# Other ranks for the planner over opening and first sweep, a shorter cost for four turns of tokens, and the second quarter of the tokens loaded second

## The chip, the cores and the metric

The kernel runs on one core of one Trainium2 chip. The metric is the device time of one execution in microseconds (us), as the median of several runs; the profile is of one execution more. The engines are TensorE (PE: matmuls and transposes), VectorE (DVE), ScalarE (ACT), GpSimd (POOL) and SyncE (SP), which here issues DMAs.

## What is computed

A two-way attention between tokens and states, and a feed-forward network over what both read:

```python
# x: 8 x 8 x 512 x 64 (batch, heads, tokens, D), state: 8 x 8 x 32 x 64, scale = 1/8
a  = softmax(scale * x @ state.T);  xread = a @ state      # tokens read states
a2 = softmax(scale * state @ x.T);  sread = a2 @ x         # states read tokens
rows = concatenate([xread, sread])                         # 8 * (512 + 32) = 4352 rows of 512
h = rows @ w_in                                            # 512 -> 2048
g = h * clip(h + 3, 0, 6) / 6
out = g @ w_out                                            # 2048 -> 512
```

Everything comes and goes as 32-bit floats; the inner products are split into parts of which three matmuls each are summed.

## The kernel before

The work is cut into units: a sweep over the eight batches b0 to b7 with the first half of the network's width, two units for all states' rows, and a second sweep over the batches with the other half. Each unit has eight steps. A step is a `first` (L1245: the matmuls L1053, for the opening's steps L1274, into a bank `ps_h`), an ACT step (`relu`, L1295), a DVE step (the product, L1298, which reads `ps_h` and so sets when that bank is free), the split of the result into a high and a low part (`g_hi` on ACT, L402, `g_lo` on DVE, L403), and later its `second` (L1343: L1053 or, unsplit, L1355), which adds into four banks `acc`.

The weights of the network arrive in two-byte pieces that are put together: a DMA at L479, a cast on ACT into `tops` (L492) and a join on DVE (L497); `w_out` is then split (L524 on ACT, L526 on DVE).

The opening does the attention of b0, since nothing can run before it. The tokens of b0 come as four quarters of two heads each, q0 to q3, on SP (`load_x`, L601), are copied into `xb` (DVE, L603), turned on TensorE (L732), copied back by ACT (L737) and multiplied with the turned states (L796): q0 and q1 into one bank of scores, q2 and q3 into another. Each bank gets a softmax on DVE and ACT: maximum L811, subtraction L813, exponential L815, sum L816, two small steps L818 and L819, scaling L820. Only when both are through does TensorE turn the result (L828), ACT copy it (L835) and the first main matmul (L1274) run. Beside it runs the states' side: `wprime` (L630, the states times `w_in`, copied by ACT at L681) and the states' own softmax (maximum L904 and L906 on DVE, exponential L908 on ACT, L911 and L913 on DVE). The tokens of the next batch come later as sixteen turned loads (`load_turned`, L617) and are transposed on DVE (L722).

What sets the order of all this is `Plan`: each operation is added with its engine, a cost, what it reads and writes and its slots. `Plan.order` (L166) then goes through time with one clock per engine, and among the operations that could start within 0.3 of the soonest it takes the one of the lowest rank. The ranks are the table `RANKS` (L25 to L132), 2592 numbers, one for each operation. `Plan.issue` (L263) emits the operations in that order, and each engine runs its own in that order on the chip. Ahead of the first main matmul it also puts idle transposes (L1660) into the gaps that TensorE has by the planned clock, one for each 0.13 of a gap. So a changed cost changes the clock, the order and the count of idle transposes.

Of the kernel before, what the change touches and what calls it, by code (L numbers as in the profile page):

```python
# [279 lines left out]
def tile_state_attention_then_hardswish_ffn(  # L280
# [72 lines left out]
    def T(cost, rank, do, reads=(), writes=(), after=()):  # L353
        return plan.add("T", cost, rank, do, reads, writes, after)
# [1336 lines left out]
```

## Time and profile before

| what | us |
|---|---|
| median of 3 runs (637.45 to 638.91) | 637.8 |
| the profiled execution | 637.48 |
| its span | 635.7 |
| TensorE busy in the span | 627.8 |
| DVE busy | 520.5 |
| ACT busy | 344.3 |

The span is the time from the first to the last instruction that the profile shows; the granted clock of TensorE is 1.00 all along. A busy TensorE has its idle transposes counted in. Waits are read from the time that an engine sat idle ahead of an instruction, with the engine and line that ended it. In timelines, matmuls of one row overlap a little, so that two starts give a better pitch than a duration does.

### The profile page before, as it was taken

The page shows a single profiled execution, that of the slowest core. Times are in us where ns is not written, and L with a number is a line of the kernel's source. Part 1 is how long each engine was busy: PE and PEld are TensorE (multiplying, and loading weights), DVE is VectorE, ACT ScalarE, POOL GpSimd, SP SyncE. Part 2 cuts the span into 40 slices and gives each one's busy share as a digit, 9 for nine tenths or more (in the row PEclk, how much of TensorE's full clock was granted, in tenths as well). Part 3 has the DMA queues.
Part 4 walks back from the last instruction along what each step waited for, and adds up shares of the span by engine and source line. Part 5 has one row for each costly group of instructions (what it writes and reads, how often), then busy time and mean ns, then how long its engine had stood idle before and what let it go on. Part 6 is the DMA issues. An engine that isn't in the chain of part 4 may idle for free.

```text
span 635.7 us, 11438 instructions
## 1 busy us (share of the span) xinstructions
PE 627.8 (99%) x4381; PEld 525.7 (83%) x4381; DVE 520.5 (82%) x947; ACT 344.3 (54%) x611; POOL 18.1 (3%) x21
## 2 busy tenths in 40 slices
PE   8999999999999999999999999999999999999997
PEld 6466777777777778778888888899999999999996
DVE  5999997978988798885568738999979899988773
ACT  5875565546545554444456657665446455554431
POOL 0000000000000000000000000000000000001010
PEclk9999999999999999999999999999999999999999
DMA  8998895966687694540313868323526225522244
GB/s 293 283 219 141 247 176 158 203 169 184 129 198 167 168 211 107 134 101 31 70 67 106 286 207 231 99 48 87 133 36 164 35 35 129 104 35 34 34 67 99
DMA packets 168261, 86.18 MB, mean 136 GB/s; under 512 B 128528, under 2 KB 152976, under 8 KB 168080
## 3 DMA queue, kind: packets, MB, share of 16 engines
q1 hardware_dynamic: 164240, 77.47, 47.3%
q0 software_dynamic: 3824, 7.87, 8.5%
q8 instruction: 34, 0.56, 0.4%
q14 instruction: 19, 0.16, 0.1%
q10 hardware_dynamic: 144, 0.13, 0.1%
HBM read 50.84 MB, written 34.60 MB: 134 GB/s over the span
## 4 chain that ended last, share of the span: by engine, by line
PE 93%; DMA 2%; DVE 2%; SPq 1%; ACT 1%; issue 0%; ACTq 0%
PE acc L1053 31%; PE acc L1165 24%; PE ps_h L1053 23%; PE ps_s L1053 7%; PE ps_s L630 2%; PE acc L1355 1%; PE ps_s L1491 1%; DMA raw<-in_moe_w_out_dram 1%; PE ps_h L1010 1%; DMA raw<-in_moe_w_in_dram 1%; SPq L617 1%; PE acc L1491 1%; PE ps_h L630 1%; DMA raw<-in_x_dram 0%; SPq L601 0%
## 5 line engine op out<-in xcount | busy, mean ns | idle before, releaser
L1053 PE MATMUL acc<-w_out_hi,g_hi 128*128 128x512 f32 x296 | 118.2, 399 | 0.5 <-ACT g_hi L402 0.5
L1053 PE MATMUL acc<-w_out_lo,g_hi 128*128 128x512 f32 x296 | 115.5, 390 | 0.0
L1053 PE MATMUL acc<-w_out_hi,g_lo 128*128 128x512 f32 x296 | 115.3, 390 | 0.0
L1165 PE MATMUL acc<-w_out_hi,tmp 128*128 128x256 f32 x360 | 87.9, 283 | 0.0
L1295 ACT ACTIVATE g<-ps_h,three 128x512 f32<-128x512 f32 (+1 forms) x80 | 51.3, 647 | 57.8 <-PE ps_h L1053 51.4
L1298 DVE SCALAR_TENSOR_TENSOR g<-g,ps_h 128x512 f32<-128x512 f32 (+1 forms) x80 | 50.1, 629 | 27.9 <-ACT g L1295 27.2
L1053 PEld LDWEIGHTS acc<-w_out_hi,g_hi 128*128 128x128 f32 x296 | 55.6, 188 | 19.6 <-issue 7.0
L1165 PE MATMUL acc<-w_out_hi,g_lo 128*128 128x256 f32 x240 | 68.0, 283 | 0.0
L1165 PE MATMUL acc<-w_out_lo,g_hi 128*128 128x256 f32 x240 | 67.9, 283 | 0.0
L1165 PE MATMUL acc<-w_out_hi,g_hi 128*128 128x256 f32 x240 | 67.9, 283 | 0.0
L1053 PE MATMUL ps_h<-aT_hi,wp_hi 128*128 128x512 f32 (+1 forms) x188 | 67.6, 360 | 0.0
L1165 PEld LDWEIGHTS acc<-w_out_hi,tmp 128*128 128x128 f32 x360 | 66.3, 192 | 0.3
L1053 PE MATMUL ps_h<-aT_lo,wp_hi 128*128 128x512 f32 (+1 forms) x188 | 66.5, 354 | 0.0
L1053 PE MATMUL ps_h<-aT_hi,wp_lo 128*128 128x512 f32 (+1 forms) x188 | 66.4, 353 | 0.0
L1053 PEld LDWEIGHTS acc<-w_out_hi,g_lo 128*128 128x128 f32 x296 | 55.6, 188 | 12.2 <-DVE g_lo L403 0.4
L1053 PEld LDWEIGHTS acc<-w_out_lo,g_hi 128*128 128x128 f32 x296 | 55.6, 188 | 10.7 <-issue 0.3
L402 ACT CAST g_hi<-G 128x512 fp32r<-128x512 f32 (+1 forms) x64 | 38.2, 605 | 46.8 <-PE acc L1165 38.7
L402 ACT CAST g_hi<-g 128x512 fp32r<-128x512 f32 (+1 forms) x74 | 42.7, 585 | 26.3 <-DVE g L1298 15.5
L403 DVE TENSOR_TENSOR g_lo<-g,g_hi 128x512 fp32r<-128x512 f32 (+1 forms) x74 | 46.8, 643 | 8.7 <-ACT g_hi L402 6.7
L1165 PE MATMUL acc<-w_out_lo,tmp 128*128 128x256 f32 x180 | 50.9, 283 | 0.0
L403 DVE TENSOR_TENSOR g_lo<-G,g_hi 128x512 fp32r<-128x512 f32 (+1 forms) x64 | 42.2, 669 | 6.1 <-ACT g_hi L402 5.5
L1165 PEld LDWEIGHTS acc<-w_out_hi,g_hi 128*128 128x128 f32 x240 | 46.0, 192 | 0.7
(179 smaller groups left out, 1272.8 us busy)
## 6 DMA issues: line engine op xcount, KB each, us to landing
out_dram<-ot SPq DMA_DIRECT2D x8, 1024.0 KB, 4.9
W<-G SPq DMA_DIRECT2D x16, 512.0 KB, 4.1
out_dram<-ot POOLq DMA_DIRECT2D x15, 512.0 KB, 5.9
raw<-in_x_dram SPq DMA_DIRECT2D x112, 64.0 KB, 2.8
xb<-in_x_dram SPq DMA_DIRECT2D x28, 256.0 KB, 4.8
raw<-in_moe_w_out_dram SPq DMA_DIRECT2D x11, 511.8 KB, 5.4
wp_lo<-W SPq DMA_DIRECT2D x40, 128.0 KB, 2.8
raw<-in_moe_w_in_dram SPq DMA_DIRECT2D x8, 511.0 KB, 5.6
```

What stands on the lines that cost most here:

```text
L402: first = S_(cost, rank, lambda: nc.scalar.copy(hi(), src()), reads, [writes[0]], after)
L403: V(cost, rank, lambda: nc.vector.tensor_tensor(lo(), src(), hi().bitcast(F32), op=ALU.subtract), [*reads, writes[0]], [writes[1]])
L617: nc.sync.dma_start(t[rows, i].rearrange("t (a c) -> t a c", c=NS), x[b, 4 * g + 2 * i + u, :, k * NS : (k + 1) * NS].rearrange("(a t) c - ...
L630: nc.tensor.matmul(out[u][cols, :], made["stT", b][rows, cols], moving(q)[rows], start=True, stop=True,)
L1010: nc.tensor.matmul(bank(pr)[cols, u * D : (u + 1) * D], e2T(b, u)[:, j * P + q * NS : j * P + (q + 1) * NS], x_tile(b, True)[:, NG * q + u ...
L1053: nc.tensor.matmul(ps, l, r, start=start and k == 0, stop=stop and k == n - 1)
L1165: nc.tensor.matmul(out, left(a, l), right(b, r), start=p == 0 and z == 0 and y == 0, stop=p == FPS // 2 - 1 and y == 2, skip_group_check=True)
L1295: in_turn["g", n] = S_(cost + 0.05, rank, lambda: nc.scalar.activation(g(), bank(ps)[:, :width], AF.Relu, bias=three, scale=-1.0 if turned ...
L1298: V(cost, rank, lambda: nc.vector.scalar_tensor_tensor(g(), g(), 6.0, bank(ps)[:, :width], op0=ALU.min, op1=ALU.mult), [ps], [g_key])
L1355: nc.tensor.matmul(bank(acc), made["g_hi", n][:, js], plain_out[f][1](), start=opens, stop=closes)
L1491: nc.tensor.matmul(bank(banks[q // 2][u])[:, q % 2 * W : (q % 2 + 1) * W], st[l]()[rows, q], wp(r)[rows, q], start=y == 0, stop=y == 2, sk ...
```

## The change

The planner's cost for the turn of a quarter of the tokens (L732) becomes 0.47 instead of 0.7, and the 2592 ranks are other ones:

```diff
 RANKS = [int(k) for k in """
-2 0 8 3 33 1 18 4 38 20 28 11 21 37 40 25 31 53 58 29 36 39 43 57
...
+10 8 82 9 97 12 100 13 94 60 98 5 160 47 170 2 169 3 181 113 107 59 4 64
...
 """.split()]
...
             x_parts = [(*x_key(b), "q", q)] if b == 0 else [(*x_key(b), j) for j in range(J)]
-            T(0.7, rank, turn, x_parts, [ps], after)
+            T(0.47, rank, turn, x_parts, [ps], after)
             S_(0.6, rank, lambda q=q, ps=ps: nc.scalar.copy(xT(b, q), bank(ps)), [ps], [xT_key(b, q)])
```

The operations are the same ones, 2592 of them, with the same instructions on DVE, ACT, SP and POOL. TensorE has eight idle transposes more, 50 instead of 42: 12, 3, 1, 7, 11, 9 and 7 in the gaps of the opening, where it had 12, 4, 1, 8, 6, 3 and 8. In the second half of the order TensorE's row is the same as before.

On SP the first quarters and the weights of the opening stand in another order. The names: `ot` is the raw tile of b0's tokens, a row of two being two quarters; `early` and `raw` are pieces of the weights. Before:

```order
L601 DMA ot<-in_x_dram 128x2x256 x2
L546 DMA st_raw<-in_state_dram 128x128
L601 DMA ot<-in_x_dram 128x2x256 x2
L479 DMA raw<-in_moe_w_out_dram 128x2047
L479 DMA early_108<-in_moe_w_in_dram 128x4x511 x2
L479 DMA early_113<-in_moe_w_in_dram 128x4x1023
L479 DMA raw<-in_moe_w_out_dram 128x2047 x2
```

After:

```order
L601 DMA ot<-in_x_dram 128x2x256 x2
L546 DMA st_raw<-in_state_dram 128x128
L479 DMA early_104<-in_moe_w_in_dram 128x4x511
L601 DMA ot<-in_x_dram 128x2x256 x2
L479 DMA raw<-in_moe_w_out_dram 128x2047 x2
L479 DMA early_104<-in_moe_w_in_dram 128x4x511
L479 DMA early_133<-in_moe_w_in_dram 128x4x1023
L479 DMA early_150<-in_moe_w_out_dram 128x2047
```

What moved: q1 now goes ahead of q2, half a piece of `w_in` goes ahead of q2 and q3, and the second piece of `w_out` comes ahead of the other pieces of `w_in`. The sixteen turned loads of the next tokens (L617), of which six went ahead of a late piece of weights, all stand behind it.

On DVE this is the opening, from the last copies L603 to the first scaling L820. `early` and `raw` at L497 are the joins of `w_in` and `w_out`, L811 to L820 the two softmaxes. Before:

```order
L603 COPY xb<-ot 128x2x4x64
L497 SCALAR_TENSOR_TENSOR raw<-raw,tops 128x512
L811 TENSOR_REDUCE m_196<-ps_s 128x16
L813 TENSOR_TENSOR w_in_204<-ps_s,m_196 128x8x64
L497 SCALAR_TENSOR_TENSOR w_in_212<-early_108,tops 128x4x128
L811 TENSOR_REDUCE m_215<-ps_s 128x16
L816 TENSOR_REDUCE s_230<-w_in_204 128x16
L813 TENSOR_TENSOR w_in_204<-ps_s,m_215 128x8x64
L818 TENSOR_SCALAR s_230<-s_230 128x16
L819 RECIPROCAL s_230<-s_230 128x16
L820 TENSOR_TENSOR w_in_204<-w_in_204,s_230 128x8x64
L816 TENSOR_REDUCE s_230<-w_in_204 128x16
```

After:

```order
L811 TENSOR_REDUCE m_180<-ps_s 128x16
L813 TENSOR_TENSOR w_in_190<-ps_s,m_180 128x8x64
L603 COPY xb<-ot 128x2x4x64
L497 SCALAR_TENSOR_TENSOR w_in_207<-early_104,tops 128x4x128
L816 TENSOR_REDUCE s_215<-w_in_190 128x16
L497 SCALAR_TENSOR_TENSOR raw<-raw,tops 128x512
L818 TENSOR_SCALAR s_215<-s_215 128x16
L819 RECIPROCAL s_215<-s_215 128x16
L497 SCALAR_TENSOR_TENSOR raw<-raw,tops 128x512
L811 TENSOR_REDUCE m_239<-ps_s 128x16
L813 TENSOR_TENSOR w_in_190<-ps_s,m_239 128x8x64
L820 TENSOR_TENSOR w_in_190<-w_in_190,s_215 128x8x64
```

What moved: the first bank's maximum and subtraction come ahead of the last copy L603, and two joins of `w_out` stand between the first bank's sum and the second bank's maximum, where before one stood ahead of everything and the other, below these rows, behind both softmaxes.

On ACT this is the end of the opening, from the copies of the turned softmax (L835) to the first two `relu` (L1295). `aT_hi` is the split of these copies, `tmp` the states' exponential. Before, with numbers:

```order
L835 COPY w_in2_204<-acc1_289 128x256
L835 COPY w_in2_204<-acc0_294 128x256
L835 COPY w_in2_204<-acc1_289 128x256
L835 COPY w_in2_204<-acc0_294 128x256
L492 CAST tops_91<-early1_113 128x512
L524 CAST w_out_hi0_228<-raw_133 128x512
L402 CAST aT_hi_327<-w_in2_204 128x512 x2
L908 ACTIVATE tmp_341,r2_342<-ps_s_248,nm2_303 128x512
L1295 ACTIVATE g_349<-ps_h_318,three_89 128x512
L908 ACTIVATE tmp_351,r2_342<-ps_s_247,nm2_299 128x512
L1295 ACTIVATE g_354<-ps_h_336,three_89 128x512
```

After:

```order
L835 COPY w_in2_190<-acc1_301 128x256 x2
L835 COPY w_in2_190<-acc0_306 128x256 x2
L402 CAST aT_hi_320<-w_in2_190 128x512
L492 CAST tops_91<-raw_167 128x512
L908 ACTIVATE tmp_341,r2_342<-ps_s_259,nm2_311 128x512
L1295 ACTIVATE g_348<-ps_h_329,three_89 128x512
L908 ACTIVATE tmp_355,r2_342<-ps_s_258,nm2_332 128x512
L492 CAST tops_91<-early3_150 128x512
L1295 ACTIVATE g_371<-ps_h_345,three_89 128x512
```

What moved: one `aT` split and the split of `w_out` no longer stand ahead of the first exponential of the states L908.

On TensorE this is the place in the first sweep where the tokens of the next batch are read (L1010): a `first` (into `ps_h`), seconds (into `acc`), the read, and then the `second` of that `first`. Before, with numbers:

```order
L1053 MATMUL ps_h_693<-aT_hi_327,wp_hi_433 128x512
L1053 MATMUL ps_h_693<-aT_lo_334,wp_hi_433 128x512
L1053 MATMUL ps_h_693<-aT_hi_327,wp_lo_446 128x512
L1053 MATMUL acc0_376<-w_out_hi1_461,g_hi_609 128x512
L1053 MATMUL acc0_376<-w_out_lo1_472,g_hi_609 128x512
L1053 MATMUL acc0_376<-w_out_hi1_461,g_lo_651 128x512
L1010 MATMUL ps_s_717<-xb_110,tmp_700 32x64 x16
L1010 MATMUL ps_s_717<-xb_110,tmp_704 32x64 x16
L1053 MATMUL acc2_370<-w_out_hi1_461,g_hi_755 128x512
L1053 MATMUL acc2_370<-w_out_lo1_472,g_hi_755 128x512
L1053 MATMUL acc2_370<-w_out_hi1_461,g_lo_759 128x512
L1053 MATMUL acc3_395<-w_out_hi1_461,g_hi_755 128x512
```

After:

```order
L1053 MATMUL ps_h_658<-aT_hi_320,wp_lo_431 128x512
L1053 MATMUL acc1_374<-w_out_hi1_513,g_hi_578 128x512
L1053 MATMUL acc1_374<-w_out_lo1_532,g_hi_578 128x512
L1053 MATMUL acc1_374<-w_out_hi1_513,g_lo_618 128x512
L1053 MATMUL acc2_386<-w_out_hi1_513,g_hi_592 128x512
L1053 MATMUL acc2_386<-w_out_lo1_532,g_hi_592 128x512
L1053 MATMUL acc2_386<-w_out_hi1_513,g_lo_602 128x512
L1053 MATMUL acc1_374<-w_out_hi1_513,g_hi_592 128x512
L1053 MATMUL acc1_374<-w_out_lo1_532,g_hi_592 128x512
L1053 MATMUL acc1_374<-w_out_hi1_513,g_lo_602 128x512
L942 MATMUL ps_s_695<-ident_84,tmp_355 128x128 x4
L942 MATMUL ps_s_700<-ident_84,tmp_341 128x128 x4
```

What moved: behind the `first` stand three seconds ahead of the turn L942 (and two more behind it, ahead of the read L1010), where before one stood between the `first` and the read; the turn was ahead of the `first`.

## Rows read from the trace of the kernel before

**Rows 1.** The page: engines (busy us, share of the span, instructions), two groups (busy, mean ns).
```profile
PE 627.8 (99%) x4381; PEld 525.7 (83%) x4381; DVE 520.5 (82%) x947; ACT 344.3 (54%) x611; POOL 18.1 (3%) x21
...
L1295 ACT ACTIVATE g<-ps_h,three 128x512 f32<-128x512 f32 (+1 forms) x80 | 51.3, 647 | 57.8 <-PE ps_h L1053 51.4
L1298 DVE SCALAR_TENSOR_TENSOR g<-g,ps_h 128x512 f32<-128x512 f32 (+1 forms) x80 | 50.1, 629 | 27.9 <-ACT g L1295 27.2
```

**Rows 2.** Busy time of each engine by stretch, granted clock, DMA share, GB/s.
```profile
10.00:20.00 10.00, 8.20 (x96) 5.84 (x95) 9.37 (x18) 7.18 (x17) 0.00 (x0) 1.00 1.02 353
...
40.00:60.00 20.00, 19.47 (x182) 13.39 (x181) 18.88 (x35) 11.99 (x21) 0.00 (x0) 1.00 0.83 168
```

**Rows 3.** TensorE's waits: us in total, times, longest us.
```profile
PE acc L630 <- DVE w_in L497: 1.1, 1, 1.1
PE acc L1053 <- ACT g_hi L402: 0.5, 1, 0.5
...
PE ps_s L630 <- ACT tmp L908: 0.2, 1, 0.2
```

**Rows 4.** The chain that ended last, to 70 us: start us, us, what.
```profile
3.23 6.34 DMA raw<-in_moe_w_out_dram
...
10.46 0.69 DVE raw L497
...
17.56 0.70 DVE w_in L820
18.31 1.11 PE acc L828 x8
```

**Rows 5.** Loads L601, half w_in, w_out1: durations ns, first and last start us; landing.
```profile
L601 SPq DMA_DIRECT2D ot<-in_x_dram x4: 431/446/469, 0.7 to 2.7; - x4
...
DMA to landing us min/median/max: 2.7/3.5/4.9
...
L479 SPq DMA_DIRECT2D early<-in_moe_w_in_dram x1: 434/434/434, 3.7 to 3.7; - x1
...
DMA to landing us min/median/max: 7.2/7.2/7.2
...
L479 SPq DMA_DIRECT2D raw<-in_moe_w_out_dram x1: 1369/1369/1369, 5.9 to 5.9; - x1
...
DMA to landing us min/median/max: 10.5/10.5/10.5
```

**Rows 6.** DVE's timeline: start us, us, line and operation, idle before.
```profile
11.78 0.69 DVE L813 TENSOR_TENSOR w_in<-ps_s,m 128x512 f32<-128x512 f32 x1
12.39 0.68 DVE L497 SCALAR_TENSOR_TENSOR w_in<-early,tops 128x512 uint32<-128x512 uint32 x1
...
14.78 0.17 DVE L818 TENSOR_SCALAR s<-s 128x16 f32<-128x16 f32 x1
...
15.27 0.69 DVE L820 TENSOR_TENSOR w_in<-w_in,s 128x512 f32<-128x512 f32 x1
```

**Rows 7.** TensorE's timeline, 16 to 32 us, same columns.
```profile
16.03 0.87 PE L1660 MATMUL ps_h<-ident 128*128 128x128 f32 x6
...
20.14 3.70 PE L1274 MATMUL ps_h<-w_in,tmp 128*128 128x512 f32 x8
23.77 0.62 PE L630 MATMUL ps_s<-w_in,stT 64*32 64x256 f32 x2
...
25.17 4.77 PE L1355 MATMUL acc<-raw,g 128*128 128x512 f32 x10
...
31.25 0.66 PE L630 MATMUL ps_s<-w_in,stT 64*32 64x256 f32 x16
```

**Rows 8.** TensorE's timeline at 59 us.
```profile
59.17 0.50 PE L1053 MATMUL acc<-w_out_hi,g_hi 128*128 128x512 f32 x1 [0.52 <-ACT g_hi L402]
...
60.25 0.40 PE L1053 MATMUL acc<-w_out_hi,g_hi 128*128 128x512 f32 x1
60.48 0.40 PE L1053 MATMUL acc<-w_out_lo,g_hi 128*128 128x512 f32 x1
```

214 rows, old and new, of the table RANKS are left out of this document.

## The prediction
> **What bounds the kernel now.** I read the page first: TensorE is busy 627.8 us of a span of 635.7 [rows 1]. So only two things can move the time by much: TensorE's own work, or the few moments in which it does no useful work. The change adds no matmul of the product and takes none away, so I looked for the moments. The busy times by stretch show the first: from 10 to 20 us TensorE is busy 8.20, and part of that is idle transposes, while DVE is busy 9.37 [rows 2]. The table of TensorE's waits then shows how little is left: 1.1 us on DVE's join of `w_in`, 0.5 on an ACT split, 0.2 on an exponential of the states [rows 3]. All three places are in the part of the order that the change rewrites, the opening and the first sweep. What is not in that table is the time that TensorE spends on idle transposes, and the time that a matmul takes longer than its neighbours while it waits in the pipeline; the timeline has to give these.
>
> The chain that ended last says what the opening hangs on: the first `w_out` load (3.23 + 6.34 = 9.57 us), DVE's join at 10.46, then DVE without a gap to the scaling of the second half's softmax at 17.56, the turn back on TensorE at 18.31 [rows 4], the first of the main matmuls at 20.14 [rows 7]. The opening is thus DVE bound from the first arriving weights on, and each 0.1 us taken out of DVE's row before 17.56 would bring TensorE's 20.14 forward by as much.
>
> **Arrivals.** Loads land in the order of issue, as their summed bytes come. With 256 KB for a quarter of the tokens, 64 for the state and 512 for a `w_out` or half `w_in` load, before gives: four quarters and the state (1,088 KB) at 2.7 + 4.9 = 7.6; + w_out0 (1,600) at 9.57; + half w_in (2,112) at 3.7 + 7.2 = 10.9; after two more `w_in` loads (512 and 1,024 KB), w_out1 (4,160) at 5.9 + 10.5 = 16.4 [rows 4, 5]. That is 2,560 KB in 6.83 us, 375 KB a us. After's order is q0, q1, state, half w_in, q2, q3, w_out0, w_out1, the other half, w_in of the next. An estimate by the same bytes: half w_in at 7.6 (1,088), q2 at 8.6 (1,344), q3 at 9.6 (1,600), w_out0 at 10.9 (2,112), w_out1 at 12.3 (2,624), the other half of w_in at 13.7 (3,136). The tokens' second half (q2, q3) comes 2 to 3 us later than before, w_out1 four earlier, and w_in's first half 3.3 earlier.
>
> This rests on order of issue deciding the landing. The Trainium skill, page "DMA: Bandwidth & Descriptors", section "Queues, rings and completion order", says that descriptors are consumed in ring order but that a later transfer may complete before an earlier one. Of the loads summed here the rows show none that did; by that rule q2 and q3 could slip towards the weights behind them, and the price would be that of rival C.
>
> **The opening on DVE.** An operation on 128x512 takes a place of 0.61 us (11.78 to 12.39), the two small ones before a scaling 0.49 together (14.78 to 15.27) [rows 6], and from a landing through ACT's cast to the join it is 0.9 (9.57 to 10.46) [rows 4]. By after's order: the first half's scores are there at about 8.7, since q0 and q1 land first, so maximum and subtraction run from 8.9 on; the copy of q3 at about 10.2; join of half w_in 10.66; sum 11.26; join of w_out0 11.87; small ones; join of w_out1 at 13.2, for which DVE waits (landing at 12.3, and 0.9); the second half's maximum 13.8, subtraction 14.4; scaling of the first 15.0; join 15.6; sum 16.2; small ones; scaling of the second 17.35 to 18.05. Before had it at 17.56 + 0.70 = 18.26 [rows 4]. So early tokens buy only 0.2 us: the row is the same work, and one more join (w_out1's) stands ahead of the end. Bounds: it could be 0.6 earlier if DVE doesn't wait for w_out1 (one place of 0.61), and later by whatever w_out1's landing is late. I take **-0.2**.
>
> The eight added idle transposes cost six for 0.87 us [rows 7], 0.14 each, 1.1 in all, if nothing covers them. What covers them is the wait for DVE: by the sum above, TensorE's row (scores of the second half, half w_in product, 11 idle, the 512-wide product, half w_in product, 9 idle) ends at about 17.9, just ahead of 18.05. I cost them at nothing, with 0.2 of cover left and 1.1 at the other end.
>
> **From 20 to 30 us.** The states' product (L630) takes 23.77 to 25.17 = 1.40 us where the same sixteen matmuls later run in 0.66 [rows 7]: 0.75 lost, of which the table names 0.2 for the exponential L908 [rows 3]. ACT comes late to that: behind the copies of the opening's end it has a cast, a split of `w_out` and both splits of `aT` ahead of L908. In after the split of `w_out` and one split of `aT` stand elsewhere. The lost 0.75 should go, so that L1355 starts 0.2 + 0.75 = **0.95 earlier**. What is late next: `aT`'s other split and the join for L630 at about 28.3; by the places of 0.6 on DVE and ACT these are done 0.1 to 0.8 ahead of use, so little cover is left. Then after has three `first` with one L1355 between the second and third, and the third needs the bank of the first, which an ACT step of 647 ns and a DVE step of 629 free [rows 1]; one queued step ahead of each makes 0.3 to 0.5 us of wait. I give back **0.3**. The sixteen turned loads of the next tokens now all stand behind a weight's buffer on SP, where six went ahead of it; their readers on DVE come about when the last of them lands, so I cost that at nothing, with 0.5, the longest stall past the opening [rows 3], at the other end.
>
> **At 59 us.** TensorE waits 0.52 for ACT's split, and the step's first three matmuls take 59.17 to 60.25 = 1.08 where one step is 0.23 (60.25 to 60.48), 0.69 for three: 0.39 more, **0.9 in all** [rows 8]. Between that `first` and its own `second` before has one other second of three matmuls and the tokens' read; after has four seconds more and the turn L942, of which the 12 matmuls alone are 12 x 0.23 = 2.8 us of cover. So this goes. But DVE, which is busy 18.88 of the 20 us up to there [rows 2], is only a little ahead of TensorE, and after puts three `first` in a row right behind. The third waits for the first one's 0.65 + 0.63, which two L1053 groups of 1.38 would hide, but DVE's backlog does not. I give back **0.5** (0.1 to 0.9).
>
> **Sum.** -0.2 - 0.75 + 0.3 - 0.9 + 0.5 = -1.05. Beyond the first sweep the order is the same: nothing. The profiled execution took 637.48, 0.3 below the median 637.8 of the three runs, of which 1.8 lie around the span; 637.48 - 1.05 = 636.4. Set against the median it would be 636.75; I put it at **636.5**. What a measurement can tell from no change is 0.2%, 1.3 us: 636.5 stands on that edge, so that "faster" and "same" share the forecast.
>
> **Rivals.**
> A. The forecast, 635.8 to 637.1: 0.50.
> B. Nothing is freed: what TensorE gains at 25 us it waits for again at 28 to 33 and at 60, since DVE is nearly as full as TensorE. For: 9.37 of 10 us, and 18.88 of 20 [rows 2], and the DVE chain in [rows 4]. Against: behind the opening TensorE's waits are waits for ACT [rows 3], not for DVE. Only the opening's 0.2 stays: 637.3 to 637.6. Chance 0.25. The Trainium skill, page "Perfetto Trace Analysis", "Engine Utilization", gives 358 GB/s as a core's share of memory and some 435 as a lone core's ceiling; the landings above come at 375 KB a us, 384 GB/s, more than the share and under the ceiling. By the share as a cap w_out1 would land 0.2 later (1,024 KB in 2.93 us instead of 2.73) and the opening's 0.2 would be gone; the rows decide against it.
> C. Slower: DVE's join of w_out1 stands in its row ahead of the second half's softmax. If w_out1, or q3, lands late, all DVE work behind it and the turn back shift one for one. It turns the sum at 1.05 us late, and comes to "slower" at 2.7. For: q2 and q3 now have 512 KB of `w_in` ahead of them, and 0.2 of cover on both engines, with 1.1 us of idle transposes behind any slip on TensorE. Against: arrival by bytes fits the rows to 0.1. With a slip of 1.8 and the idle transposes of 1.1 uncovered: 637.5 - 1.05 + 2.9 = 639.3. Chance 0.13.
> D. Everything is freed: the 0.8 given back isn't, and DVE does not wait for w_out1 (0.6): 637.5 - 1.05 - 1.4 = 635.0. Chance 0.12.
>
> **How the numbers follow.** The range takes A and D's upper half and B, and C's smaller slips: 635.3 to 638.2; outside lie half of D and most of C, some 0.18. Faster by over 0.2% (under 636.5): half of A, and D: 0.25 + 0.12, with 0.01 by rounding: 0.38. Same: the other half of A, most of B, and C's smaller slips: 0.49. Slower (over 639.1): C, 0.13.
>
> **What would show it.** The scores' maximum L811 at about 8.9 and the last scaling L820 at 17.35; L1274 at about 19.9; L630 in 0.7 and L1355 at about 24.2; no wait for g_hi at 59, and instead waits of ps_h on L1298 around 33 and 65. L1274 later than 20.2 makes C; L1355 at 24.2 and unchanged times at 60 makes B. The prediction is wrong if TensorE's waits in 20 to 70 us grow over 1 us, or if a new one stands past 70, where I moved nothing by hand.

## The result, and the profile after

The changed kernel takes 644.57 us (median of 4 runs, 644.07 to 645.09), the kernel before 637.62 on the same chip (4 runs, 637.26 to 638.91): a ratio of 1.0103, with a 95% interval of 1.0088 to 1.0118. It is 7 us slower, where 636.5 was forecast; the time lies far above the range of 635.3 to 638.2.

The changed kernel's profiled execution has a span of 643.1. Its table of TensorE's waits answers to [rows 3] (us in total, times, longest us):

```profile
PE ps_h L1053 <- DVE g L1298: 4.3, 1, 4.3
...
PE ps_s L709 <- DMA st_raw<-in_state_dram: 1.0, 1, 1.0
PE ps_h L1053 <- DVE wp_lo L403: 0.6, 1, 0.6
...
PE acc L1053 <- DVE g_lo L403: 0.4, 1, 0.4
PE acc L630 <- ACT tops L492: 0.2, 1, 0.2
```

The waits of before are gone as forecast: 1.1 for the join, 0.5 for `g_hi`, 0.2 for the exponential. In their place stands one wait of 4.3 us, longer than all of them. Busy times by stretch show where (as in [rows 2]: PE, PEld, DVE, ACT, POOL busy, granted clock, DMA share, GB/s):

```profile
70.00:76.00 6.00, 6.00 (x99) 4.12 (x97) 2.61 (x5) 0.69 (x1) 0.00 (x0) 1.00 0.38 96
76.00:80.60 4.60, 0.32 (x2) 0.00 (x0) 2.52 (x5) 3.03 (x5) 0.00 (x0) 1.00 1.02 380
80.60:84.30 3.70, 3.67 (x10) 2.84 (x11) 3.67 (x8) 1.09 (x3) 0.00 (x0) 0.57 1.28 229
84.30:88.00 3.70, 3.70 (x17) 3.06 (x16) 3.52 (x9) 2.31 (x6) 0.00 (x0) 0.97 1.41 171
```

From 76.0 to 80.6 TensorE does next to nothing, and for the 3.7 us behind that the granted clock is 0.57 of full speed, nearly all of it at the lower of the two levels (1.2 GHz): another 3.7 x 0.43 = 1.6 us. The timelines of the four engines tell why. SP, DVE, ACT and TensorE of the changed kernel, each with start us, us, operation and the idle time before it:

```profile
63.62 0.84 SPq L981 DMA_DIRECT2D raw<-e  x1
72.64 0.35 SPq L479 DMA_DIRECT2D raw<-in_moe_w_out_dram  x1
```

```profile
71.91 0.70 DVE L722 STREAM_TRANSPOSE tmp<-raw 128x512 f32<-128x512 f32 x1
78.08 1.29 DVE L403 TENSOR_TENSOR g_lo<-g,g_hi 128x512 fp32r<-128x512 f32 x2 [5.47 <-ACT g_hi L402]
79.29 0.69 DVE L497 SCALAR_TENSOR_TENSOR raw<-raw,tops 128x512 uint32<-128x512 uint32 x1
79.89 0.68 DVE L1298 SCALAR_TENSOR_TENSOR g<-g,ps_h 128x512 f32<-128x512 f32 x1
```

```profile
76.81 0.76 ACT L492 CAST tops<-raw 128x512 f16<-128x512 bf16 x1 [5.54 <-DMA raw<-in_moe_w_out_dram]
77.44 1.12 ACT L402 CAST g_hi<-g 128x512 fp32r<-128x512 f32 x2
78.87 0.69 ACT L1295 ACTIVATE g<-ps_h,three 128x512 f32<-128x512 f32 x1 [0.30 <-DVE g_lo L403]
```

```profile
75.93 0.39 PE L1053 MATMUL acc<-w_out_hi,g_lo 128*128 128x512 f32 x1
80.63 0.50 PE L1053 MATMUL ps_h<-aT_hi,ot 128*128 128x512 f32 x1 [4.31 <-DVE g L1298]
...
82.98 0.63 PE L1053 MATMUL acc<-w_out_hi,g_hi 128*128 128x512 f32 x1
83.41 0.63 PE L1053 MATMUL acc<-w_out_lo,g_hi 128*128 128x512 f32 x1
```

Read backwards: a `first` on TensorE waits at 80.63 for its bank, which the product L1298 frees at 80.6; DVE had stood idle for 5.47 us behind the splits `g_hi`; these stood on ACT behind a cast L492, and the cast waited 5.54 us for a load. The load is a piece of `w_out` of which nothing in this sweep is made (it is for the other half of the width). SP issued it at 72.64, just when DVE's second transpose L722 ended (71.91 + 0.70 = 72.61), and it landed 4.2 us later. In the kernel before the same load went 8 us earlier:

```profile
64.48 0.49 SPq L479 DMA_DIRECT2D raw<-in_moe_w_out_dram  x1
```

So the load, by this reading, waited for a buffer that the turned tokens held; the experiments test that.

In the stretch of the lower granted clock, matmuls of one row start 0.43 us apart (82.98 to 83.41), against the 0.23 of [rows 8]. The Trainium skill, page "TensorE: Matmul & The Clock Gate", section "Wait — 56ns, not 53.3ns?", gives 426.7 ns for N = 512 at 1.2 GHz; the trace agrees.

The opening, which answers to [rows 7]:

```profile
6.66 0.46 PE L709 MATMUL ps_s<-ident,st_raw 128*64 128x64 f32 x8 [0.96 <-DMA st_raw<-in_state_dram]
...
19.20 1.10 PE L828 MATMUL acc<-ident,w_in 128*128 128x128 f32 x8
...
21.15 3.70 PE L1274 MATMUL ps_h<-w_in,tmp 128*128 128x512 f32 x8
24.78 0.66 PE L630 MATMUL ps_s<-w_in,stT 64*32 64x256 f32 x16
25.37 4.77 PE L1355 MATMUL acc<-raw,g 128*128 128x512 f32 x10
```

The first main matmul starts at 21.15 instead of 20.14, but the states' product L630 takes 0.59 (24.78 to 25.37) instead of 1.40, so that L1355 is only 0.2 later than in [rows 7].

### The profile page after: what moved, and what is told of

It reads as the page before. It is cut to its first block, busy times and chain, and to the rows that moved or that the text cites. A ratio compares the mean times of both kernels' runs of the same rounds, so it can differ in the third digit from the quotient of the medians.

```text
span 643.1 us, 11456 instructions
## 1 busy us (share of the span) xinstructions
PE 630.2 (98%) x4389; PEld 527.4 (82%) x4389; DVE 519.7 (81%) x947; ACT 344.6 (54%) x611; POOL 18.1 (3%) x21
## 4 chain that ended last, share of the span: by engine, by line
PE 90%; DVE 4%; DMA 2%; ACT 1%; issue 1%; SPq 1%; DVEq 0%
PE acc L1053 29%; PE acc L1165 24%; PE ps_h L1053 23%; PE ps_s L1053 7%; PE ps_s L630 2%; PE ps_s L1491 1%; PE acc L1491 1%; PE acc L1355 1%; PE ps_h L1010 1%; PE ps_h L630 1%; SPq L617 1%; DMA st_raw<-in_state_dram 1%; DMA raw<-in_moe_w_out_dram 1%; PE ps_h L1274 1%; DVE tmp L722 1%
## 5 line engine op out<-in xcount | busy, mean ns | idle before, releaser
L1295 ACT ACTIVATE g<-ps_h,three 128x512 f32<-128x512 f32 (+1 forms) x80 | 51.2, 645 | 52.5 <-PE ps_h L1053 49.4
L1298 DVE SCALAR_TENSOR_TENSOR g<-g,ps_h 128x512 f32<-128x512 f32 (+1 forms) x80 | 50.0, 629 | 29.8 <-ACT g L1295 28.9
L1053 PEld LDWEIGHTS acc<-w_out_hi,g_hi 128*128 128x128 f32 x296 | 55.8, 189 | 18.7 <-issue 3.9
L1053 PEld LDWEIGHTS acc<-w_out_lo,g_hi 128*128 128x128 f32 x296 | 55.9, 189 | 11.1 <-issue 0.5
L403 DVE TENSOR_TENSOR g_lo<-g,g_hi 128x512 fp32r<-128x512 f32 (+1 forms) x74 | 46.5, 642 | 21.6 <-ACT g_hi L402 18.6
L403 DVE TENSOR_TENSOR g_lo<-G,g_hi 128x512 fp32r<-128x512 f32 (+1 forms) x64 | 42.1, 668 | 6.1 <-ACT g_hi L402 5.5
L1165 PEld LDWEIGHTS acc<-w_out_lo,g_hi 128*128 128x128 f32 x240 | 46.0, 192 | 0.7
```

Source lines behind the costliest of these rows:

```text
L403: V(cost, rank, lambda: nc.vector.tensor_tensor(lo(), src(), hi().bitcast(F32), op=ALU.subtract), [*reads, writes[0]], [writes[1]])
L1053: nc.tensor.matmul(ps, l, r, start=start and k == 0, stop=stop and k == n - 1)
L1165: nc.tensor.matmul(out, left(a, l), right(b, r), start=p == 0 and z == 0 and y == 0, stop=p == FPS // 2 - 1 and y == 2, skip_group_check=True)
L1295: in_turn["g", n] = S_(cost + 0.05, rank, lambda: nc.scalar.activation(g(), bank(ps)[:, :width], AF.Relu, bias=three, scale=-1.0 if turned ...
L1298: V(cost, rank, lambda: nc.vector.scalar_tensor_tensor(g(), g(), 6.0, bank(ps)[:, :width], op0=ALU.min, op1=ALU.mult), [ps], [g_key])
```

## The experiments

The late load was the first theory; the rivals were the three `first` in a row with DVE's backlog, as in the prediction, and for the opening either the state's load or the arrival of q2 and q3. The first four runs:

**The buffers as planned.** The planner gives every raw tile one of three buffers and orders by that; the kernel asks the pool for a tile of the one name, and the pool gives what buffer it will. In the changed kernel the planner had the `w_out` piece in the buffer that the moved blocks of the states left at 61 us, and the pool gave it that of the turned tokens. The edit makes the name follow the plan; it stands at all six places where a raw tile is made:

```diff
+    raw_at = lambda key, shape, dtype: get(key, lambda: stage.tile(shape, dtype, name="raw", tag=f"raw{plan.home[key[:2]]}", bufs=1))
...
-                return get(place, lambda: stage.tile([P, 512, 2], U32, name="raw")).unsqueeze(1)
+                return raw_at(place, [P, 512, 2], U32).unsqueeze(1)
```

> The changed kernel with one edit: each raw tile is made in the buffer that the planner gave it, instead of any of the pool's three. All four engines' orders stay as they are. Theory 1 (the late weight): at 72.6 us the load of a w_out piece that only the second sweep needs waited for a buffer that two DVE transposes held, its cast stood on ACT ahead of two g_hi splits and a relu, and TensorE waited 4.3 us and then ran at half clock for some 4 us. With the planned buffer the load goes at 64 to 65 us, no wait over 1 us is left at 76 to 81, the granted clock stays 1.00, and the time falls by 4.3 + 1.7 = 6.0 to 638.6 (637.8 to 639.4). Rival (three firsts in a row with DVE's backlog make the wait, the load is beside the point): the 4.3 us stay, 644.5.

Measured: 637.55 us, a ratio to before of 0.999 (0.9975 to 1.0004). All four engines run the same rows in the same order as in the changed kernel. SP's timeline and the waits of this run:

```profile
61.78 0.92 SPq L981 DMA_DIRECT2D raw<-e  x1
62.74 1.14 SPq L479 DMA_DIRECT2D raw<-in_moe_w_out_dram  x1
...
71.14 0.38 SPq L479 DMA_DIRECT2D raw<-in_moe_w_in_dram  x1
```

```profile
PE ps_h L1053 <- DVE wp_lo L403: 0.6, 1, 0.6
...
PE acc L630 <- DVE w_in L497: 0.2, 1, 0.2
```

The load goes at 62.74, the wait of 4.3 and the lower clock are gone, and with them the whole 7 us, where 6.0 were expected. The rival falls: the three `first` in a row are still there. The edit gives some other raw tiles another buffer too (the `w_in` piece at 71.14 went at 74.51 in the changed kernel), so it doesn't single out the one load; the next run and the reverse below bear on that.

**The cast behind.** The buffers are left, and the load stays late; only the places of its cast on ACT and of its join on DVE are moved, by names of the planner's operations:

```diff
-            for n in self.order(RANKS):
+            for n in moved(self.order(RANKS)):
...
+MOVES = [(474, 336), (475, 337)]   # cast L492 behind the relu, join L497 behind the product
```

> The changed kernel with the buffers as they were, but the cast of the late w_out piece moved on ACT behind the two g_hi splits and the relu that it held up, and its join on DVE behind the next product L1298. Theory 1 says that the lateness costs only by the place in ACT's row: the load still goes at 72.6 and lands at 76.8, but TensorE's 4.3 us wait and the half clock are gone: 638.5 to 639.8. If something else needs the load itself, or if the wait comes from DVE's backlog, 643 to 644.5.

Measured: 640.49 us, ratio 1.0035 (1.0018 to 1.0052). ACT and DVE:

```profile
74.31 1.14 ACT L402 CAST g_hi<-g 128x512 fp32r<-128x512 f32 x2 [0.76 <-DVE g L1298]
75.76 0.69 ACT L1295 ACTIVATE g<-ps_h,three 128x512 f32<-128x512 f32 x1 [0.30 <-DVE g_lo L403]
79.08 0.77 ACT L492 CAST tops<-raw 128x512 f16<-128x512 bf16 x1 [2.64 <-DMA raw<-in_moe_w_out_dram]
```

```profile
74.97 1.29 DVE L403 TENSOR_TENSOR g_lo<-g,g_hi 128x512 fp32r<-128x512 f32 x2
76.48 0.69 DVE L1298 SCALAR_TENSOR_TENSOR g<-g,ps_h 128x512 f32<-128x512 f32 x1 [0.21 <-ACT g L1295]
79.89 0.69 DVE L497 SCALAR_TENSOR_TENSOR raw<-raw,tops 128x512 uint32<-128x512 uint32 x1 [2.72 <-ACT tops L492]
```

The splits and the product no longer wait for the load, and 4 of the 7 us are back. The rest, more than expected, is in the main the same thing one row further: the join at 79.89 waits 2.72 us, and everything behind it on DVE with it; TensorE waits 1.6 us for the step L1019 that stands there. Compared with the planned buffers by the matmuls that are left (as under *Size of it* below), 1.8 us are lost there, with the matmuls that start slowly behind the wait, 0.6 at a wait for a product L1298 at 89.64, and 2.8 in all behind the load; between the medians it is 2.9. A late load costs by the rows of two engines, not by one. (The profiled execution took 643.95, 3.5 above the median, the slowest of the ten. Its first main matmul starts at 23.43, 2.3 later than in the changed kernel, and the times above are that much later.)

**The opening.** Two edits of the order on SP, the buffers as in the changed kernel:

```diff
+MOVES = [(0, 1)]    # after_state_second: the state's load behind q0
...
+MOVES = [(48, 7)]   # after_win_behind: the early half piece of w_in behind q3
```

> The changed kernel with the load of the state moved one place forward on SP, behind the first quarter of tokens instead of behind the second. Theory 2 (the opening): the state landed at 6.62 us where before had 5.26, and with it the states' turn, the scores and the first main matmul (21.15 instead of 20.14) came 1.0 later. Moved forward it should land by 4.5 and the first main matmul start at 20.1 to 20.4; the time falls by 0.7 to 1.0, to 643.6 to 643.9. Rival (the opening is bound by DVE and by the arrival of q2 and q3, not by the state): first main matmul at 20.9 or later, 644.3 to 644.7.

> The changed kernel with the early half piece of w_in put behind q2 and q3 on SP, so that the state again has tokens behind it as in the kernel before. If the small state load was late because 511 KB of w_in came into the same rings behind it, it lands at about 5.3 and q2, q3 about 1.4 us earlier, so that the first main matmul starts at 20.0 to 20.4 and the time is 643.5 to 643.9. If a lull in the transfers at 4 to 6 us is there whatever is loaded, the state is late again or another load is, 644.3 to 644.8.

Measured: 645.04 us (1.0097, 1.007 to 1.0125) and 644.75 (1.0092, 1.0064 to 1.012): no gain from either. With the state second it landed at 3.9, but then q1 landed at 6.6 and the first main matmul started at 20.98. With the half piece behind, the state landed at 5.65 and the first main matmul started at 20.47, 0.7 earlier than in the changed kernel. Its end is no earlier; in the profiled execution the gain is lost at the wait. Busy times of that run, columns as above:

```profile
75.00:79.50 4.50, 0.59 (x3) 0.15 (x1) 2.38 (x4) 2.89 (x5) 0.00 (x0) 0.90 1.01 374
79.50:85.00 5.50, 5.33 (x13) 4.17 (x14) 5.20 (x13) 2.31 (x6) 0.00 (x0) 0.50 1.30 235
```

The wait is as long (4.1 us), but behind it come 5.5 us at a granted clock of 0.50 instead of 3.7 at 0.57, 2.75 against 1.6 us. So as long as the wait is there, a small gain ahead of it needn't reach the end.

**The reverse, in the kernel before.** All orders as in the kernel before, planned buffers, but those of two pieces exchanged, so that the `w_out` piece gets the buffer of the turned tokens:

```diff
+SWAP = {("raw", ("out", 8)): ("raw", ("in", 10)), ("raw", ("in", 10)): ("raw", ("out", 8))}
```

> The kernel before, all orders as they are, with two raw buffers exchanged: the w_out piece for the second sweep gets the buffer that the two DVE transposes of the next tokens hold until 71.45 us, and the w_in piece gets the one that was free at 64. Theory 1 (it is the buffer, not the order): the load goes at 71.5 instead of 64.5 and lands at about 75.6; here its cast stands behind the g_hi splits and its join behind the product, as in the run with the cast behind, so DVE idles some 2.5 us and the time rises by 2 to 3.5, to 639.9 to 641.4. Rival (the loss needs the changed order of the engines): 637.5 to 638.2.

Measured: 640.87 us, ratio 1.0043 (1.0024 to 1.0061): 2.8 us slower without a change to any engine's order.

```profile
73.76 0.33 SPq L479 DMA_DIRECT2D raw<-in_moe_w_out_dram  x1
```

```profile
78.32 0.69 DVE L497 SCALAR_TENSOR_TENSOR raw<-raw,tops 128x512 uint32<-128x512 uint32 x1 [2.33 <-ACT tops L492]
```

The load goes at 73.76, just behind a transpose L722 that ends at 73.03 + 0.70 = 73.73, and the join idles DVE for 2.33. In the kernel before it was the `w_in` piece that went just behind that transpose (71.49, behind 70.75 + 0.70 = 71.45). That the late load costs 7 us in the changed kernel and 2.8 here fits the place of cast and join in the rows, which here stand behind the splits and the product.

The profile bears out the size only in part. It is of the slowest of the five executions (642.5), its span is 5.0 us longer than that of the kernel before, and 2.3 of these lie ahead of the late load: 1.4 at 61.44, where TensorE waits 1.89 us instead of 0.52 for a split that comes after a DVE wait of 1.46 for turned tokens, and the rest at 44 and 50. The other 2.8 lie behind the load, 1.4 of them at 82.72, where TensorE waits for the step L1019 behind the join. Whether the first 2.3 come from the edit or from this execution is not shown, and the kernel before with planned buffers that are not exchanged was not run.

**The parts of the change alone.** The one cost with the old ranks, and the new ranks with the old cost:

```diff
 # before_cost047: the kernel before
-            T(0.7, rank, turn, x_parts, [ps], after)
+            T(0.47, rank, turn, x_parts, [ps], after)
...
 # after_cost07: the changed kernel
-            T(0.47, rank, turn, x_parts, [ps], after)
+            T(0.7, rank, turn, x_parts, [ps], after)
```

> The kernel before with the one cost of the change alone: 0.47 for the token turns, the ranks as before. The planner's clock then makes another order from the first turn on. If the ranks carry the change, this is a neighbour of the kernel before without a search, 637 to 642; what it tells is whether the w_out piece again gets a late buffer: if its load goes behind 70 us, TensorE's waits at 70 to 85 us add up to 2 us or more; if it goes at 65 or earlier there are none.

> The changed kernel with the old cost of 0.7 and the new ranks. Order and buffers are made anew by planner and pool. If the time goes with the buffer, it is 644 or more with a load behind 70 us and a wait of 3 us or more on TensorE, and 639 or less with a load at 65 or earlier; if the new ranks are slow for another reason, it is 643 or more with the load early.

Measured: 638.14 us (1.0001, 0.9988 to 1.0013) and 670.06 (1.0506, 1.0478 to 1.0535). The cost alone makes another order that is as good, with the load at 64.68. The new ranks with the old cost lose 32 us, and not by the late load, which goes at 58.27 there:

```profile
PE acc L1053 <- ACT g_hi L402: 5.3, 3, 2.2
PE ps_h L1053 <- DVE ot L403: 4.8, 1, 4.8
PE ps_s L942 <- DVE tmp L881: 3.1, 1, 3.1
PE ps_h L1053 <- DVE wp_lo L403: 2.1, 2, 1.6
```

The waits are many and spread, some 20 us in all behind the start, and the granted clock is 0.60 from 108 to 125 us: ranks tuned for one clock of the planner are, here, no ranks for another. The parts can't be priced apart.

**What is left: the wait at 66.** With the planned buffers TensorE still waits 0.6 us for a bank that the split `wp_lo` (L403) frees. Three runs:

```diff
+MOVES = [(287, 304)]           # after_homes_wplo: by a slip back, behind the second product L1298
...
+MOVES = [(287, 210)]           # after_homes_split_early: ahead of L1383 and L911 to L1019
...
+MOVES = [(287, 210), (48, 7)]  # after_homes_win_behind: that, and the half piece of w_in behind q3
```

> The changed kernel with the planned buffers, and one move more: the split wp_lo (DVE, L403) that frees a ps_h bank goes ahead of the two steps L1383 and L911 to L1019, since TensorE still waited 0.6 us for that bank at 66. If the wait is on DVE's place for that one step, it goes, and the time falls by 0.4 to 0.7 against the planned buffers alone, to 636.9 to 637.2. Rival (the next first waits for the same DVE row instead): no difference, 637.3 to 637.7.

Measured: 640.37 us, ratio 1.0029 (1.002 to 1.0039). The expectation is for a move forward; this kernel has the split two products later, by a slip of mine. What it shows is the other side:

```profile
66.63 0.50 PE L1053 MATMUL ps_h<-aT_hi,ot 128*128 128x512 f32 x1 [1.56 <-DVE g L1298]
...
69.84 0.50 PE L1053 MATMUL ps_h<-aT_hi,ot 128*128 128x512 f32 x1 [1.56 <-DVE g L1298]
```

Two waits of 1.56 us for products in place of one of 0.6 for the split. The split now reads its bank from 69.71 to 70.39, and the second of the two matmuls starts at 69.84, before that: it doesn't wait for the split's own bank, but for the one that the product L1298 leaves at 69.79, and the first of the two in the same way (66.58). My reading is that one bank, held by the split for longer, is missing there; it was not tested.

> The changed kernel with the planned buffers once more, in five rounds, beside the next two and the kernel before on the same chip: the first measurement left open whether the change without the late load is a gain (interval 0.9975 to 1.0004). The forecast's -1.05 us would be 0.9984; no gain is 1.000. By the trace the opening and the place at 59 give 0.5 to 1.0 and the wait at 66 takes 0.6 back: 0.9985 to 0.9998.

> The planned buffers, and the split wp_lo (DVE, L403) that frees a ps_h bank really put forward, ahead of L1383 and L911 to L1019; in the run named after_homes_wplo it had by a slip been put back, behind the second product L1298, so that run shows the other direction: two waits of 1.56 us and 2.8 us lost. Forward, TensorE's wait of 0.6 us at 66 should go: 0.4 to 0.7 us less than the planned buffers alone. Rival: the next first waits on the same DVE row instead, no difference.

> As the run before (planned buffers, split put forward), and the early half piece of w_in behind q2 and q3 on SP. In the run with that load order alone the state, q2 and q3 landed 1 to 2.4 us earlier and the first main matmul came at 20.47 instead of 21.15, but the longer half clock behind the wait at 76 swallowed it. Without that wait it should show: 0.2 to 0.7 us less than the run before, 635.9 to 636.9 if the median of before is 637.9. Rival (the opening's start varies by as much from run to run, and DVE's row sets it): no difference.

Measured beside each other: 637.9 us (0.9994, 0.9979 to 1.0008), 638.03 (1.0, 0.9983 to 1.0016) and 637.54 (0.999, 0.9978 to 1.0002). Put forward, the split's wait goes and one of 0.5 us for the product comes, further on in the row:

```profile
68.42 0.50 PE L1053 MATMUL ps_h<-aT_hi,ot 128*128 128x512 f32 x1 [0.47 <-DVE g L1298]
```

That is the rival: DVE's row is full there, and the next bank waits on it instead. The third kernel has the lowest median, 0.6 us under before and 0.5 under the run with the split alone, with an interval that still touches 1. None of the versions is shown to beat the kernel before.

## Why the prediction was wrong

**The step that failed** is how far the sum reaches. Its terms are the opening, 20 to 30 us, and the place at 59 with the three `first` right behind it. For all that follows it has one line, "Beyond the first sweep the order is the same: nothing". That line holds: from 315.2 us of the changed kernel and 307.8 of the kernel before TensorE's row is the same, and the same 327.9 us remain. But from 66 us to there, still in the first sweep, the rows differ too, and this stretch the sum put at nothing without a term or a reason. The 7 us stand in it, at 76 to 88.

Two things had moved there that the prediction didn't read. The load of the `w_out` piece got another buffer, which no row names, and went at 72.64 instead of 64.48; the prediction had followed a buffer once only, for the turned tokens' loads. And the piece's cast and join stand ahead of the splits and of the product; in the kernel before they stood behind, on ACT like this:

```profile
70.87 1.15 ACT L402 CAST g_hi<-g 128x512 fp32r<-128x512 f32 x2 [0.76 <-DVE g L1298]
72.31 0.69 ACT L1295 ACTIVATE g<-ps_h,three 128x512 f32<-128x512 f32 x1 [0.30 <-DVE g_lo L403]
72.90 0.79 ACT L492 CAST tops<-raw 128x512 f16<-128x512 bf16 x1
```

The prediction priced this kind of thing in rival C (a weight's load late, with all of DVE behind it, chance 0.13), and said that a new wait past 70 would make it wrong. C had the mechanism, but for another load, at another place; its 639.3 is short too, since C had a slip and no lower clock.

**Size of it.** The changed kernel and that with the planned buffers run the same matmuls in the same order, so a place in them can be named by the TensorE instructions that are left behind it, as the stretches count them. With 4,200 left (at L1355, 26.0 us in the changed kernel) 617.1 us of its span remain, and 610.2 of the other's; with 3,812 left (75.9) 567.2 and 561.0; with 3,786 left (88.0) 555.1 in both. So of the 7.7 us between the spans (643.1 and 635.4), 0.8 lie in the opening, with a state's load that landed 0.8 later; 0.7 between 26 and 75.9, of which 0.4 is the wait for `g_lo`; and 6.2 between 75.9 and 88: the wait of 4.3, the 1.6 of lower clock, and 0.3 that no row places. Nothing is lost behind 88. (Both are single executions; the medians are 7.0 apart.)

**Arrivals: right.** Forecast for the loads in after's order 7.6, 8.6, 9.6, 10.9, 12.3 and 13.7; the changed kernel's landed at 8.0, 8.75, 9.5, 10.7, 12.1 and 13.5.

**The opening on DVE: the sum of its row right, a term left out.** The forecast had the first maximum at 8.9, the last scaling at 17.35 and the first main matmul at 19.9. The changed kernel had 10.12, 18.45 and 21.15. The term is the state's own load, which the prediction never priced: the first scores need it, and now they come first. The state's load and the first main matmul, in us, in the profiles with this opening (without the run with the cast behind, where TensorE ran slow: 6.4 and 23.43):

| run | state landed | first main matmul |
|---|---|---|
| after_homes_wplo | 4.6 | 19.89 |
| after_homes_again | 5.1 | 19.97 |
| after_homes | 5.8 | 20.36 |
| after | 6.6 | 21.15 |
| after_homes_split_early | 6.6 | 21.16 |

With the state by 5.1 the forecast holds step by step: in after_homes_again the first maximum starts at 8.90, the last scaling at 17.28 and the first main matmul at 19.97. In the order of the kernel before, whose scores come later, a state at 5.3 gave 20.14 and one at 5.9 gave 19.96 (before_late_load). So in these profiles the change made the time of the first main matmul vary by 1.3 us with one small load, on which it had not visibly hung before.

**The eight idle transposes: right.** L828 starts at 19.20, behind the scaling that ends at 18.45 + 0.69 = 19.14; they are covered, by 0.1 (the last of them ends at 17.86 + 1.20 = 19.06).

**From 20 to 30 us: right.** From the first main matmul to L1355 it is 4.22 us in place of 5.03 [rows 7], 0.81 less where 0.75 was forecast, and the same 4.22 in each run of this opening; in after_homes_again L1355 starts at 24.2, as forecast. The wait that I gave back 0.3 for, of the third `first` at 33, didn't come.

**At 59: right, and what took its place was mis-sized.** The wait for `g_hi` [rows 3] is gone in after; 0.4 for `g_lo` came in some runs. At 66 the wait of 0.6 came where 0.5 was given back, but for a bank held by a split, not for the first product: about the size, by another cause.

**The forecast without the late load** was -1.05 us, 0.9984. Measured with planned buffers: 0.999 and 0.9994, -0.4 to -0.6 us. Both intervals hold 1 and also the forecast's 0.9984, so that neither a gain nor its absence is shown.

**Left open:** by which rule the pool chose the tokens' buffer for this load, and why the small load early in the opening lands up to 2 us apart from run to run.

## What to carry to other kernels

When a planner orders by buffers that it gives out itself, make the built program use these very buffers, or look up which buffer each load got: two programs whose engines run the same rows in the same order were 7 us apart here. A load that is needed late can still be the most expensive one, by the rows of the engines that its cast and its join stand in. And a wait of 4 us on TensorE had a price behind its end too, which can swallow a gain made ahead of it; behind the wait of 1.6 us in the run with the cast behind the granted clock stayed at 1.00.

## What of the hardware was not expected

Behind nearly equal waits, 4.3 and 4.1 us, the lower clock cost 1.6 us in the changed kernel and 2.75 with the half piece behind. The length of the wait doesn't explain that. What differs is when the clock fell: in the changed kernel it stood at 1.00 until TensorE was at work again (0.55 from 81 to 82 us, the wait ends at 80.6); with the half piece behind it had fallen before the wait ended (0.79 from 78 to 79, the wait ends at 79.7), and with the state second too (0.73 from 78 to 79, the wait ends at 80.2).

In the run with the cast behind, the opening's scores of q0 and q1 took 3.51 us, against 1.97 for the same sixteen matmuls in the changed kernel, and seven idle transposes behind them 1.57 against 0.93, while the profile's column of the granted clock stands at 1.00:

```profile
8.59 3.51 PE L796 MATMUL ps_s<-sread_t,w_in 128*128 128x64 f32 x16
```

```profile
8.00:14.00 6.00, 6.00 (x30) 6.00 (x29) 2.26 (x5) 2.04 (x4) 0.00 (x0) 1.00 1.04 386
```

So a clock of 1.00 in that column doesn't say that TensorE ran at its full pace; the pitch of its matmuls does. What slowed it there the trace doesn't show.

And whichever small load was third or second, the transfers slackened between 3.5 and 4.5 us: 126 GB/s with the state second, 197 in the changed kernel, 218 in the kernel before, against 269 to 361 in the microsecond ahead of it; least with the half piece behind, 281 against 345. In the first two the load issued at 1.74 landed at 6.6, which was the state in the changed kernel and q1 where the state had gone ahead. The cause is open.

```profile
2.50:3.50 1.00, 1.00 (x6) 1.00 (x6) 0.00 (x0) 0.00 (x0) 0.00 (x0) 1.00 0.81 269
3.50:4.50 1.00, 1.00 (x6) 0.61 (x5) 0.43 (x1) 0.00 (x0) 0.00 (x0) 1.00 0.53 126
4.50:5.50 1.00, 1.00 (x6) 1.00 (x5) 0.00 (x0) 0.17 (x1) 0.00 (x0) 1.00 0.79 212
```
